# A list planner's cost table and rank offsets replaced: the same instructions of a fused Fourier filter and gated unit in another order

## The chip, the cores and the metric

The kernel runs on one NeuronCore of a Trainium2 chip. The metric is device time in microseconds (us) of one execution, as the median of several. A core has a matrix engine (TensorE, PE in the profile), a vector engine (VectorE, DVE), a scalar engine for activations (ScalarE, ACT), a general engine (GpSimd, POOL) that here starts the loads, and a queue engine (SyncE, SP) that here starts all other transfers. Each engine works off its own list of instructions in the order in which they were written and waits on semaphores; 16 DMA engines move the data. TensorE writes into PSUM, 128 partitions wide; VectorE and ScalarE empty it.

## The reference

Input x has 8 batches of 3200 positions by 256 channels. The first half is a circular filter along the positions, through a real Fourier transform; the second half a causal convolution of five taps per channel, whose sigmoid gates a projection:

```python
X = np.fft.rfft(x, axis=1)
y = np.fft.irfft(X * (filt_r + 1j * filt_i), n=3200, axis=1)
gate = sigmoid(sum(conv_w[k] * y_padded[:, k:k + S, :] for k in range(5)))
out = (gate * (y @ w_val)) @ w_out
```

## The kernel before, in words

The transform of 3200 points is done as 100 times 32, with small matrix products. Per batch the work is cut into these tasks, and a name such as `s1` 2,3 means task 3 of batch 2. In the changed kernel every line number is one higher.

- `lx` (8 per batch): POOL starts a load of 200 KB of x into one of ten buffers (line 200).
- `s1` (8, line 467): PE, transform over 100; `so`: VectorE or ScalarE empties the PSUM tile (lines 458 on ScalarE and 460 on VectorE; these two lines serve `so`, `xs`, `ue` and `oe`).
- `t` (4, line 486): VectorE transposes in blocks of 32.
- `s2` (7, line 496): PE, transform over 32; `xs`: emptied by either engine; `z` (7, line 512): VectorE multiplies by the filter; `ia` (7, line 527): PE, inverse over 32; `ue`: emptied by either engine.
- `wr` (7, line 550) and `lv` (8, lines 560 and 561): SP writes the result to a scratch tensor in DRAM, `escr`, and reads it back as tile `vt`, with rows and partitions exchanged. Every `lv` of a batch waits for all seven `wr` of the batch. Batch 0 alone does this with VectorE transposes instead (`k`, line 568).
- `ib` (8, line 578): PE, inverse over 100; `ye` (8, line 587): ScalarE empties it into `yt`.
- `cv` (7, line 627; the last, quarter-wide one line 613): PE, the convolution as five diagonal products. It needs all eight `ye` of its batch. Two neighbouring pieces are one task with two PSUM slots. `ga` (7, line 637): ScalarE, sigmoid.
- `vl` (7, line 647): PE, the projection; `gv` (7, line 662): VectorE, gate times projection; `op` (7, line 670): PE, the output projection; `oe`: emptied by either engine; `st` (7, line 685): SP stores 512 KB.

The last `s2`, `xs`, `z`, `ia` and `ue` task of a batch is half as wide, the last `cv`, `ga`, `vl`, `gv`, `op`, `oe` and `st` a quarter as wide. PSUM has four slots of this size, and each PE task holds one (a pair of `cv` two) until it is emptied. There are four `gt` and four `gv` buffers, four output buffers, one `u`, one `vt`.

What order the tasks have is not written by hand. A planner (class `Plan`) lists all tasks with the engine and time that each is reckoned to take, their dependencies, buffers and a rank, and lets the time run: whenever an engine is free, the ready task of the lowest rank takes it, and a task that two engines can do goes to whichever takes it. The rank is made of the tables `LAG`, `FIRST` and `STEP`:

```python
return t0 + LAG[stage] + (FIRST.get(stage, 0) if b == 0 else 0) + STEP.get(stage, 1) * n
```

with `t0` eight times the batch number. `STAY` is added for PE when a task has another shape of tiles than the last, and `LEAN` for VectorE when ScalarE could do the task too. Transfers are tasks on an engine `DQ` of their own, in the order in which they become ready, taking turns between loads and the rest. The reckoned times only decide the order; in the finished program every engine waits for the real semaphores.

Of the kernel before, what the change touches and what calls it, by code (L numbers as in the profile page):

```python
# [20 lines left out]
NV = 4 * NS  # L21
TURN = (0,)

LAG = dict(lx=-196.5, s1=-215.5, so=-54.5, t=9.5, pd=-50, s2=-219, xs=-44.5, z=193.5, ia=60,
           ue=52.5, k=-194, ib=97, ye=-272, cv=79.5, ga=-241.5, vl=-22, gv=-253.5, op=152,
           oe=-151)
FIRST = dict(lx=-125.5, s1=102, so=31.5, t=257, pd=29, s2=41, xs=-256, z=-217, ia=-4.5, ue=25,
             k=20.5, ib=113, ye=135, cv=-14.5, ga=-103.5, vl=78, gv=-43.5, op=126, oe=145)
CONV = 1.14
STEP = dict(lx=0, s1=2.15, so=0.4, t=0.4, pd=0.3, s2=1.9, xs=0.4, z=0.8, ue=0.2, k=2.2, ib=2.45,  # L30
            ye=0.5, cv=2.4, ga=2, vl=1.15, gv=1.9, op=1.35, oe=0)
STAY, LEAN = 30.5, 87.5
RC = 4
NCH = R // RC
UCH = [(m, min(2, NM - m)) for m in range(0, NM, 2)]
# [104 lines left out]
def kernel(  # L140
# [28 lines left out]
    DQ = D // E  # L169
# [22 lines left out]
    st = {}  # L192
# [4 lines left out]
    def load_x(b, j):  # L197
        xt = xpool.tile([128, RC, D], BF16, name="xt")
        src = x[b].rearrange("(a r) d -> a r d", r=R)[:, RC * j:RC * j + RC, :]
        nc.gpsimd.dma_start(out=xt[0:L], in_=src)  # L200
        st["X", b, j] = xt
# [490 lines left out]
    add = plan.add  # L692
# [1 line left out]
    def two(a, v):  # L694
        return {"ACT": a, "DVE": v}

    def dma(name, us, rank, dep, give=(), land=2.0):
        add(name, {"DQ": us}, rank, dep, None, land=land, mode=0)
        add(name + "+", {"none": 0.0}, rank, [name], None, give=give)

    for b in range(B):
        turned = b in TURN
        t0 = NCH * b

        def at(stage, n=0, b=b, t0=t0):
            return t0 + LAG[stage] + (FIRST.get(stage, 0) if b == 0 else 0) + STEP.get(stage, 1) * n

        for j in range(NCH):
            if b:
                add(f"lx{b},{j}", {"POOL": 0.6}, at("lx", j), ["hold"],  # L710
                    lambda e, b=b, j=j: load_x(b, j), take=("xt",), land=1.5)
                add(f"dx{b},{j}", {"DQ": 1.15}, at("lx", j), [f"lx{b},{j}"], None, land=2.0, mode=1)
            dep = [f"dx{b},{j}"] if b else [f"x0{j}", "cfa"]
            dep = dep + ([f"s1{b},{j - 1}"] if j else [])
            add(f"s1{b},{j}", {"PE": 0.45}, at("s1", j), dep, lambda e, b=b, j=j: s1(b, j),
                ps=1, take=("so",) if j == 0 else (), give=("xt",), mode=0)
            add(f"so{b},{j}", two(0.93, 1.14), at("so", j), [f"s1{b},{j}"],
                lambda e, b=b, j=j: so(b, j, e), free=[(f"s1{b},{j}", 0)])
        for q in range(4):
            add(f"t{b},{q}", {"DVE": 1.17}, at("t"), [f"so{b},{j}" for j in range(NCH)]  # L720
                + ([f"t{b},{q - 1}"] if q else []),
                lambda e, b=b, q=q: turn(b, q), take=("t",) if q == 0 else (),
                give=("so",) if q == 3 else ())
        add(f"pd{b}", {"POOL": 1.2} if turned else {"none": 0.0}, at("pd"),
            ["pool"] + ([f"pd{b - 1}"] if b else []),
            lambda e, b=b: pad(b), take=("u",) if turned else ("u", "e"))
        for u, (m0, nm) in enumerate(UCH):
            half = 0 if m0 + nm <= FCUT[0][1] else 1
            add(f"s2{b},{u}", {"PE": 0.11 * nm}, at("s2", u), ["wa"]
                + [f"t{b},{q}" for q in range(4)] + ([f"s2{b},{u - 1}"] if u else []),  # L730
                lambda e, b=b, u=u: s2(b, u), ps=1, take=("xs", "z"),
                give=("t",) if u == len(UCH) - 1 else (), mode=1)
            add(f"xs{b},{u}", two(0.13 + 0.4 * nm, 0.04 + 0.55 * nm), at("xs", u),
                [f"s2{b},{u}"], lambda e, b=b, u=u: xs(b, u, e), free=[(f"s2{b},{u}", 0)])
            add(f"z{b},{u}", {"DVE": 0.06 + 0.55 * nm}, at("z", u), [f"xs{b},{u}", f"fl{half}"],
                lambda e, b=b, u=u: zed(b, u), give=("xs",))
            add(f"ia{b},{u}", {"PE": 0.22 * nm}, at("ia", u),
                [f"z{b},{u}", f"te{u // 2},1", f"pd{b}"],
                lambda e, b=b, u=u: inva(b, u), ps=1, give=("z",), mode=1)
            add(f"ue{b},{u}", two(0.13 + 0.4 * nm, 0.04 + 0.55 * nm), at("ue", u),  # L740
                [f"ia{b},{u}"], lambda e, b=b, u=u: ue(b, u, e), free=[(f"ia{b},{u}", 0)])
            if not turned:
                add(f"wr{b},{u}", {"SP": 0.45}, at("ue", u), [f"ue{b},{u}"],
                    lambda e, b=b, u=u: wr(b, u), land=1.0)
                dma(f"wq{b},{u}", 0.38 * nm, at("ue", u), [f"wr{b},{u}"])
        if turned:
            for q in range(4):
                add(f"k{b},{q}", {"DVE": 1.87}, at("k"), [f"ue{b},{u}" for u in range(len(UCH))]
                    + ([f"k{b},{q - 1}"] if q else []),
                    lambda e, b=b, q=q: back(b, q), take=("v",) if q == 0 else (),  # L750
                    give=("u",) if q == 3 else ())
        else:
            add(f"wd{b}", {"none": 0.0}, at("ue"), [f"wq{b},{u}+" for u in range(len(UCH))],
                None, take=("v",), give=("u",))
            for j in range(NCH):
                add(f"lv{b},{j}", {"SP": 0.8}, at("ib", j) - 2, [f"wd{b}"],
                    lambda e, b=b, j=j: lv(b, j), land=1.0)
                dma(f"lq{b},{j}", 0.6, at("ib", j), [f"lv{b},{j}"])
        for j in range(NCH):
            add(f"ib{b},{j}", {"PE": 0.37}, at("ib", j),  # L760
                [f"k{b},3" if turned else f"lq{b},{j}+", "cim"]
                + ([f"ib{b},{j - 1}"] if j else []),
                lambda e, b=b, j=j: ib(b, j), ps=1, take=("y",) if j == 0 else (),
                give=(("v",) if turned else ("v", "e")) if j == NCH - 1 else (), mode=0)
            add(f"ye{b},{j}", {"ACT": 0.79}, at("ye", j), [f"ib{b},{j}"],
                lambda e, b=b, j=j: ye(b, j), free=[(f"ib{b},{j}", 0)])
        add(f"ha{b}", {"POOL": 0.2}, at("ib"), [f"ye{b},0"], lambda e, b=b: halo(b))
        for c in range(NB):
            f = width(c) / BLK
            if c == NB - 1:  # L770
                add(f"cv{b},{c}", {"PE": 0.28}, at("cv", c),
                    [f"ye{b},{j}" for j in range(NCH)] + [f"ha{b}", "dg0", "dg1"],
                    lambda e, b=b, c=c: conv(b, c), ps=1, take=("g",), mode=1)
            elif c % 2 == 0:
                add(f"cv{b},{c}", {"PE": CONV}, at("cv", c),
                    [f"ye{b},{j}" for j in range(NCH)] + [f"ha{b}", "dg0", "dg1"],
                    lambda e, b=b, c=c: conv(b, c), ps=2, take=("g", "g"), mode=2)
            p = c // 2 * 2
            add(f"ga{b},{c}", {"ACT": 0.77 * f + 0.16}, at("ga", c), [f"cv{b},{p}"],
                lambda e, b=b, c=c: gate(b, c), free=[(f"cv{b},{p}", c % 2)])  # L780
            add(f"vl{b},{c}", {"PE": 0.87 * f}, at("vl", c),
                [f"cv{b},{p}"] + ([f"vl{b},{c - 1}"] if c else []), lambda e, b=b, c=c: val(b, c),
                ps=1, take=("gv",), give=("y",) if c == NB - 1 else (), mode=0)
            add(f"gv{b},{c}", {"DVE": 1.08 * f + 0.06}, at("gv", c),
                [f"vl{b},{c}", f"ga{b},{c}"], lambda e, b=b, c=c: gv(b, c), give=("g",),
                free=[(f"vl{b},{c}", 0)])
            add(f"op{b},{c}", {"PE": 0.88 * f}, at("op", c), [f"gv{b},{c}"],
                lambda e, b=b, c=c: outp(b, c), ps=1, take=("o",), give=("gv",), mode=0)
            add(f"oe{b},{c}", two(0.77 * f + 0.16, 1.08 * f + 0.06), at("oe", c),
                [f"op{b},{c}"], lambda e, b=b, c=c: oe(b, c, e), free=[(f"op{b},{c}", 0)])  # L790
            add(f"st{b},{c}", {"SP": 0.5}, at("oe", c), [f"oe{b},{c}"],
                lambda e, b=b, c=c: store(b, c), land=1.0)
            dma(f"sq{b},{c}", 1.2 * f, at("oe", c), [f"st{b},{c}"], give=("o",))
    add("pool", {"none": 0.0}, -100, [], None, land=20.0)
    add("wts", {"POOL": 5.0}, 8.5, ["hold"], lambda e: load_w())
    for j in range(NCH):
# [65 lines left out]
```

## Time and profile before

| what | value |
|---|---|
| three runs | 312.55, 313.03 and 317.41 us; median 313.03 |
| the profiled execution | 311.8 us |
| its span | 310.0 us, so 1.8 us lie around the span |
| mean granted TensorE clock | 0.963 |
| instructions in the span | 10810 |
| HBM | 42.54 MB read, 38.14 MB written |

Busy time of an engine is the time in which some instruction of it runs. Two instructions that follow each other without a pause overlap a little, so the step from one to the next is shorter than the duration of one. The DMA share is the mean busy share of the 16 DMA engines.

### The profile page before, as it was taken

The page shows a single profiled execution, that of the slowest core. Times are in us where ns is not written, and L with a number is a line of the kernel's source. Part 1 is how long each engine was busy: PE and PEld are TensorE (multiplying, and loading weights), DVE is VectorE, ACT ScalarE, POOL GpSimd, SP SyncE. Part 2 cuts the span into 40 slices and gives each one's busy share as a digit, 9 for nine tenths or more (in the row PEclk, how much of TensorE's full clock was granted, in tenths as well). Part 3 has the DMA queues.
Part 4 walks back from the last instruction along what each step waited for, and adds up shares of the span by engine and source line. Part 5 has one row for each costly group of instructions (what it writes and reads, how often), then busy time and mean ns, then how long its engine had stood idle before and what let it go on. Part 6 is the DMA issues. An engine that isn't in the chain of part 4 may idle for free.

```text
span 310.0 us, 10810 instructions
## 1 busy us (share of the span) xinstructions
PE 253.6 (82%) x4616; PEld 157.5 (51%) x4644; DVE 265.0 (85%) x294; ACT 244.9 (79%) x291; POOL 59.4 (19%) x123
## 2 busy tenths in 40 slices
PE   2832779788986799998959969999899989899992
PEld 0121516344544535664547336655666556667661
DVE  7789898899896979999979968999999999285672
ACT  3963889997895888899959957997878789869652
POOL 8773658510230032002300400000000000000000
PEclk9999986999997699999999998999999999999998
DMA  6998699999799969957999978963874789785656
GB/s 98 182 188 157 101 174 123 165 194 239 252 220 243 326 147 239 289 205 171 196 276 327 241 145 266 293 224 118 259 242 164 270 261 294 260 286 191 262 221 237
DMA packets 53520, 67.79 MB, mean 219 GB/s; under 512 B 7840, under 2 KB 34336, under 8 KB 53472
## 3 DMA queue, kind: packets, MB, share of 16 engines
q1 hardware_dynamic: 41264, 51.79, 50.3%
q0 software_dynamic: 12208, 15.31, 31.0%
q8 instruction: 36, 0.59, 0.7%
q14 instruction: 12, 0.10, 0.1%
HBM read 42.54 MB, written 38.14 MB: 260 GB/s over the span
## 4 chain that ended last, share of the span: by engine, by line
PE 34%; DMA 23%; DVE 20%; ACT 8%; issue 7%; POOL 4%; SPq 2%; DVEq 0%; ACTq 0%; POOLq 0%
DMA vt<-escr 9%; PE ps L647 8%; PE ps L670 8%; DMA xt<-in_x_dram 7%; PE ps L627 7%; DVE z L512 6%; DVE gv L662 5%; PE ps L578 4%; PE ps L527 3%; DVE tt L486 3%; PE ps L467 3%; POOL xt L200 2%; ACT gt L637 2%; DVE xs L460 2%; DMA f_t<-in_filt_i_dram 2%
## 5 line engine op out<-in xcount | busy, mean ns | idle before, releaser
L662 DVE TENSOR_TENSOR gv<-ps,gt 128x1024 bf16<-128x1024 f32 (+1 forms) x56 | 61.1, 1103 | 13.0 <-PE ps L647 11.2
L637 ACT ACTIVATE gt<-ps 128x1024 bf16<-128x1024 f32 (+1 forms) x56 | 50.0, 935 | 18.2 <-PE ps L627 16.8
L512 DVE TENSOR_TENSOR z<-xs,f_t 128x2048 bf16<-128x2048 bf16 (+1 forms) x56 | 62.6, 1141 | 0.5 <-ACT xs L458 0.2
L587 ACT ACTIVATE yt<-ps 128x800 bf16<-128x800 f32 x64 | 51.8, 851 | 8.2 <-PE ps L578 5.9
L670 PE MATMUL ps<-wo_t,gv 128*128 128x256 bf16 x400 | 52.0, 274 | 6.5 <-issue 5.2
L200 POOL DMA_DIRECT2D xt<-in_x_dram x64 | 35.4, 557 | 100.8 <-PE ps L467 93.1
L467 PE MATMUL ps<-xt,cf_t 100*128 100x512 bf16 x128 | 44.0, 433 | 12.3 <-DMA xt<-in_x_dram 8.0
L647 PE MATMUL ps<-yt,wv_t 128*128 128x512 bf16 (+1 forms) x196 | 51.4, 356 | 2.2 <-ACT gt L637 0.4
L458 ACT ACTIVATE u<-ps 128x1024 bf16<-128x1024 f32 (+1 forms) x39 | 39.0, 1009 | 12.2 <-PE ps L527 7.9
L670 PEld LDWEIGHTS <-gv 128*128 128x128 bf16 x400 | 37.5, 98 | 16.3 <-issue 9.3
L458 ACT ACTIVATE so<-ps 128x1024 bf16<-128x1024 f32 x39 | 38.8, 1040 | 5.7 <-PE ps L467 5.3
L486 DVE STREAM_TRANSPOSE tt<-so 128x1024 f32<-128x1024 f32 x32 | 39.0, 1234 | 2.0 <-ACT so L458 2.0
L578 PE MATMUL ps<-ci_t,vt 104*128 104x100 f16 (+1 forms) x512 | 35.0, 219 | 7.1 <-DMA vt<-escr 5.2
L458 ACT ACTIVATE xs<-ps 128x1024 bf16<-128x1024 f32 (+1 forms) x38 | 35.9, 975 | 5.5 <-PE ps L496 5.0
L527 PE MATMUL ps<-z,a_t 64*64 64x256 bf16 x416 | 30.5, 309 | 9.7 <-DVE z L512 9.0
L627 PE MATMUL ps<-yt,dg_t 32*32 32x512 bf16 x1920 | 35.9, 387 | 3.1 <-issue 1.3
L578 PEld LDWEIGHTS <-vt 104*128 104x128 bf16 (+1 forms) x512 | 29.3, 104 | 16.7 <-DMA vt<-escr 6.5
L458 ACT ACTIVATE o<-ps 128x1024 f32<-128x1024 f32 (+1 forms) x34 | 32.7, 973 | 6.2 <-PE ps L670 5.0
L460 DVE CAST so<-ps 128x1024 bf16<-128x1024 f32 x25 | 30.1, 1226 | 3.5 <-PE ps L467 3.2
L460 DVE COPY o<-ps 128x1024 f32<-128x1024 f32 (+1 forms) x22 | 22.7, 1033 | 12.0 <-PE ps L670 12.0
L627 PEld LDWEIGHTS <-dg_t 32*32 32x32 bf16 x1920 | 24.1, 88 | 14.5 <-issue 11.0
L496 PE MATMUL ps<-tt,w_t 64*64 64x256 bf16 x416 | 22.8, 298 | 8.8 <-DVE tt L486 5.8
(98 smaller groups left out, 209.6 us busy)
## 6 DMA issues: line engine op xcount, KB each, us to landing
out_dram<-o SPq DMA_DIRECT2D x48, 512.0 KB
xt<-in_x_dram POOLq DMA_DIRECT2D x64, 200.0 KB, 7.7
escr<-u SPq DMA_DIRECT2D x42, 256.0 KB
vt<-escr SPq DMA_DIRECT2D x56, 192.0 KB
out_dram<-o SPq DMA_DIRECT2D x8, 128.0 KB
f_t<-f_t SPq DMA_DIRECT2D x4, 224.0 KB
escr<-u SPq DMA_DIRECT2D x7, 128.0 KB
vt<-escr SPq DMA_DIRECT2D x56, 16.0 KB
```

Of the source, the lines that this page charges most:

```text
L458: nc.scalar.activation(dst, src, AF.Copy, **kw)
L460: nc.vector.tensor_copy(dst, src)
L467: nc.tensor.matmul(ps[:, 512 * h:512 * h + 512], lhsT=cf_t[0:L].rearrange("p h c i -> p (h c i)"), rhs=xv[:, DQ // 2 * h:DQ // 2 * h + DQ ...
L486: nc.vector.transpose(dst, src)
L512: nc.vector.tensor_tensor(z[:, :, :, 0:nm * D], st.pop(("XS", b, u))[:, :, 0:nm * D].unsqueeze(1) .to_broadcast((128, 2, 2, nm * D)), f_t[ ...
L578: nc.tensor.matmul(ps[:, o:o + L], lhsT=v[rows, RC * j + a, 128 * dh:128 * dh + 128], rhs=ci_t[rows, way, :], start=True, stop=True)
L587: nc.scalar.activation(y[:, :, H:H + N].rearrange("p h (a r) -> p h a r", r=R)[:, :, :, RC * j:RC * j + RC], ps[:, :].rearrange("p (h n) - ...
L627: nc.tensor.matmul(two[s][o:o + 32, 512 * dh:512 * dh + BLK], lhsT=dg_t[rows, dh, k, 32 * (i % 2):32 * (i % 2) + 32], rhs=y[rows, dh, p:p ...
L637: nc.scalar.activation(g[:, :, 0:w], two_banks(ps, w), AF.Sigmoid)
L647: nc.tensor.matmul(ps[:, 512 * eh:512 * eh + w], lhsT=wv_t[:, dh, eh, o:o + 128], rhs=y[:, dh, H + BLK * c:H + BLK * c + w], start=(dh == ...
L662: nc.vector.tensor_tensor(o, i0, i1, op=ALU.mult)
L670: nc.tensor.matmul(ps[:, D * a:D * a + D], lhsT=gv_[:, eh, 128 * a:128 * a + 128], rhs=wo_t[:, c % 2, eh, :], start=(eh == 0), stop=(eh == 1))
```

## The change

Nothing is added or taken away: the same matmuls, tiles, loads and stores. The cost table of the planner gets other times for transfers (a load 1.22 instead of 1.15, `wr` 0.44 per half instead of 0.38, `lv` 0.68 instead of 0.6, a store 1.35 instead of 1.2, landing 2.3 instead of 2.0), `CONV` is 1.2 instead of 1.14, and all offsets are other numbers:

```diff
-LAG = dict(lx=-196.5, s1=-215.5, so=-54.5, t=9.5, pd=-50, s2=-219, xs=-44.5, z=193.5, ia=60,
-           ue=52.5, k=-194, ib=97, ye=-272, cv=79.5, ga=-241.5, vl=-22, gv=-253.5, op=152,
-           oe=-151)
-FIRST = dict(lx=-125.5, s1=102, so=31.5, t=257, pd=29, s2=41, xs=-256, z=-217, ia=-4.5, ue=25,
-             k=20.5, ib=113, ye=135, cv=-14.5, ga=-103.5, vl=78, gv=-43.5, op=126, oe=145)
-CONV = 1.14
-STEP = dict(lx=0, s1=2.15, so=0.4, t=0.4, pd=0.3, s2=1.9, xs=0.4, z=0.8, ue=0.2, k=2.2, ib=2.45,
-            ye=0.5, cv=2.4, ga=2, vl=1.15, gv=1.9, op=1.35, oe=0)
-STAY, LEAN = 30.5, 87.5
+LAG = dict(lx=-483.5, s1=-502, so=-78.5, t=229.5, pd=-88, s2=-43.5, xs=8.5, z=246.5, ia=176.5,
+           ue=177.5, k=-247.5, ib=250.5, ye=-415, cv=169, ga=-359, vl=-112.5, gv=-318.5, op=258,
+           oe=-181)
+FIRST = dict(lx=-97.5, s1=161.5, so=44.5, t=431, pd=68.5, s2=193, xs=-429.5, z=-282, ia=9,
+             ue=10.5, k=218.5, ib=167.5, ye=240, cv=25.5, ga=-153, vl=175, gv=-64.5, op=293.5,
+             oe=245)
+CONV = 1.2
+STEP = dict(lx=0.15, s1=2.35, so=1.55, t=1.9, pd=2.2, s2=1.45, xs=2.5, z=1.5, ia=0.2, ue=2.1,
+            k=0, ib=0.3, ye=1.85, cv=0.45, ga=0.85, vl=2.4, gv=0.1, op=1.65, oe=2.05)
+STAY, LEAN = 32.5, 120.5
...
-    def dma(name, us, rank, dep, give=(), land=2.0):
-        add(name, {"DQ": us}, rank, dep, None, land=land, mode=0)
+    def dma(name, us, rank, dep, give=(), land=2.3, mode=0):
+        add(name, {"DQ": us}, rank, dep, None, land=land, mode=mode)
...
-                add(f"dx{b},{j}", {"DQ": 1.15}, at("lx", j), [f"lx{b},{j}"], None, land=2.0, mode=1)
+                add(f"dx{b},{j}", {"DQ": 1.22}, at("lx", j), [f"lx{b},{j}"], None, land=2.0, mode=1)
...
-                dma(f"wq{b},{u}", 0.38 * nm, at("ue", u), [f"wr{b},{u}"])
+                dma(f"wq{b},{u}", 0.44 * nm, at("ue", u), [f"wr{b},{u}"])
...
-                dma(f"lq{b},{j}", 0.6, at("ib", j), [f"lv{b},{j}"])
+                dma(f"lq{b},{j}", 0.68, at("ib", j), [f"lv{b},{j}"])
...
-            dma(f"sq{b},{c}", 1.2 * f, at("oe", c), [f"st{b},{c}"], give=("o",))
+            dma(f"sq{b},{c}", 1.35 * f, at("oe", c), [f"st{b},{c}"], give=("o",))
```

What the planner makes of it, as it stands in the built programs. Up to the end of `ib` of batch 0 (PE), of `t` of batch 1 (VectorE) and of `ye` of batch 0 (ScalarE) both orders are the same. Then the changed order does `s2` and `ia` of batch 1 before the first `cv` of batch 0 is over. From the first `cv` of batch 1 it repeats itself, four times without any difference (digits are task numbers; `cv`, `vl`, `op` and their followers are of batch b, `ib` and `ye` of b+1, `s2` to `ue` of b+2, `s1`, `so` and `t` of b+3, for b = 1 to 4):

```
PE   cv:0 s1:0 vl:0 s1:1 vl:1 s1:2 s2:0 s1:3 s2:1 s1:45 s2:2 s1:67 cv:24 ia:0 s2:3 ia:12 s2:45 op:0
     ib:0 vl:2 ib:1 op:1 ia:3 vl:3 s2:6 cv:6 ia:4 ib:2 op:2 ib:3 vl:4 ia:5 ib:4 op:3 ib:5 vl:5 ib:6
     op:4 ia:6 vl:6 ib:7 op:56
DVE  so:0 gv:01 xs:012 z:012 ue:0 xs:3 ue:2 xs:5 z:3 gv:2 z:4 gv:3 t:0 z:5 oe:2 gv:4 t:1 z:6 gv:5 t:2
     gv:6 t:3 oe:6
ACT  ga:01 so:1234567 ga:2345 ue:1 xs:4 oe:0 ye:01 oe:1 ue:3 xs:6 ga:6 ue:4 ye:23 ue:5 ye:4 oe:3 ye:56
     oe:4 ue:6 ye:7 oe:5
SP   lv:01234567 (b+1) wr:012 st:01 wr:34 st:2 wr:5 st:34 wr:6 st:65
```

Before, no two batches had the same order, and SP's list mixed `lv` of one batch with `wr` and `st` of others. The loads of x for batch b+4 follow `s1` of b+3 in both. Two tasks fall out of the pattern: `op` 0,5 and `op` 0,6 of batch 0 now come at the very end (after `op` 5,3 and after `op` 7,6), and until then their inputs hold two of the four `gv` buffers.

Which engine empties PSUM changes too:

| emptied by | `so` | `xs` | `ue` | `oe` | all |
|---|---|---|---|---|---|
| VectorE, before | 25 | 18 | 17 | 22 | 82 |
| VectorE, after | 9 | 31 | 15 | 20 | 75 |
| ScalarE, before | 39 | 38 | 39 | 34 | 150 |
| ScalarE, after | 55 | 25 | 41 | 36 | 157 |

## The prediction

> **What bounds the kernel now.** The page first: who is busy, what the transfers cost, what the chain of the end is made of.
>
> ```profile
> span 310.0 us, 10810 instructions
> ...
> PE 253.6 (82%) x4616; PEld 157.5 (51%) x4644; DVE 265.0 (85%) x294; ACT 244.9 (79%) x291; POOL 59.4 (19%) x123
> ...
> q1 hardware_dynamic: 41264, 51.79, 50.3%
> q0 software_dynamic: 12208, 15.31, 31.0%
> ...
> PE 34%; DMA 23%; DVE 20%; ACT 8%; issue 7%; POOL 4%; SPq 2%; DVEq 0%; ACTq 0%; POOLq 0%
> ```
>
> No engine is full over the whole span, and the chain is a third transfers and VectorE together with a third TensorE: a pipeline whose bound changes. So I cut the span where both orders have a landmark: the end of the last common stretch, the first `cv` of batch 1, that of batch 4, that of batch 5.
>
> ```profile
> core 0: us, PE busy (x) PEld busy (x) DVE busy (x) ACT busy (x) POOL busy (x), PEclk, DMA share, GB/s
> 0.00:54.30 54.30, 32.07 (x316) 15.91 (x316) 45.59 (x89) 38.56 (x54) 36.55 (x76) 0.94 0.90 146
> 54.30:106.30 52.00, 41.47 (x724) 24.92 (x727) 46.07 (x43) 44.25 (x50) 10.04 (x20) 0.93 0.96 233
> 106.30:213.80 107.50, 95.09 (x1760) 57.48 (x1764) 98.98 (x94) 91.30 (x107) 12.60 (x26) 0.97 0.82 224
> 213.80:239.60 25.80, 23.93 (x556) 16.75 (x566) 25.60 (x24) 20.80 (x27) 0.10 (x1) 1.00 0.67 226
> 239.60:310.00 70.40, 61.00 (x1302) 42.49 (x1279) 48.74 (x48) 49.98 (x58) 0.10 (x1) 0.98 0.72 252
> ```
>
> Four regimes. From 54 to 106 the DMA engines are at 0.96 and nobody else is full. From 106 to 214 VectorE is 92% busy (98.98 of 107.5), with 8.5 us idle. To 239.6 it is full (25.60 of 25.80). Behind that TensorE leads (61.0 of 70.4) and VectorE idles 21.7 us. What VectorE waits for in the two middle regimes shows in the chain:
>
> ```profile
> 84.90 10.54 DMA vt<-escr
> ...
> 146.72 4.43 DMA escr<-u
> 151.17 5.90 DMA vt<-escr
> 157.09 6.71 DMA vt<-escr
> 164.16 3.25 DMA vt<-escr
> ```
>
> Twice the round trip through the scratch tensor holds the chain: 10.5 us from 84.9, 20.3 us in four pieces from 146.7. The landmarks themselves:
>
> ```profile
> 107.06 2.36 PE L627 MATMUL ps<-yt,dg_t 32*32 32x512 bf16 x80
> ...
> 239.27 1.40 PE L627 MATMUL ps<-yt,dg_t 32*32 32x512 bf16 x80
> ```
>
> Batch 1's `cv` starts at 107.1, batch 5's at 239.3; 132.2 us lie between them and 70.7 behind.
>
> **The change, stage by stage.** The work is the same, so the sums need the step of an instruction when its engine is never idle. VectorE's from a stretch without a pause:
>
> ```profile
> 48.69 4.62 DVE L486 STREAM_TRANSPOSE tt<-so 128x1024 f32<-128x1024 f32 x4 [1.16 <-ACT so L458]
> ...
> 205.58 0.67 DVE L512 TENSOR_TENSOR z<-xs,f_t 128x1024 bf16<-128x1024 bf16 x1
> 206.17 1.21 DVE L460 CAST so<-ps 128x1024 bf16<-128x1024 f32 x1
> ...
> 208.43 0.41 DVE L662 TENSOR_TENSOR gv<-ps,gt 128x256 bf16<-128x256 f32 x1
> 208.76 1.22 DVE L512 TENSOR_TENSOR z<-xs,f_t 128x2048 bf16<-128x2048 bf16 x1
> ...
> 219.68 1.21 DVE L460 CAST u<-ps 128x1024 bf16<-128x1024 f32 x1
> 220.81 1.22 DVE L460 CAST xs<-ps 128x1024 bf16<-128x1024 f32 x1
> ```
>
> From 219.68 to 220.81 is 1.13 us, and four transposes in 4.62, the last of them 1.2, give the same: 1.13 for a full tile, whatever the operation; a half `z` steps 0.59 (205.58 to 206.17), a quarter tile 0.33. ScalarE's:
>
> ```profile
> 162.58 0.59 ACT L458 ACTIVATE xs<-ps 128x512 bf16<-128x512 f32 x1
> 163.05 1.03 ACT L458 ACTIVATE u<-ps 128x1024 bf16<-128x1024 f32 x1
> ...
> 268.70 1.94 ACT L637 ACTIVATE gt<-ps 128x1024 bf16<-128x1024 f32 x2 [0.31 <-PE ps L627]
> ...
> 279.79 3.10 ACT L587 ACTIVATE yt<-ps 128x800 bf16<-128x800 f32 x4
> ```
>
> A full tile steps 0.92 (1.94 for two, the second ending 1.02 after its start), a `ye` 0.75 (3.10 less a last 0.84, by three), a half tile 0.47; for a quarter I take 0.33 as on VectorE.
>
> *To 53.3 us* nothing differs on any engine: the four `t` of batch 1 end at 48.69 + 4.62.
>
> *53.3 to the first `cv` of batch 1.* The changed order gives VectorE 40 full tiles, two halves and a quarter here: 40 x 1.13 + 2 x 0.59 + 0.33 = 46.7. Without a pause that ends at 100.0; at the 88.6% of today (46.07 of 52.0) at 106.0. ScalarE has 37 full tiles, eight `ye`, four halves and a quarter: 42.3, so it is not the bound. What can go is the wait of 10.54. Today three stores of batch 0 stand on SP ahead of the first `lv` of batch 1 and a fourth between them; now it is one. A store is 0.524 MB, and the hardware queue moved 51.79 MB in 0.503 x 310.0 = 155.9 us of all engines, 3.01 us per MB: 1.58 per store, three of them 4.7 us. The last `ue` of batch 1 also comes ahead of `ga` 0,2 and 0,3 instead of behind them, so the last `wr` starts no later. The loads of x stay where they are, and they hold most of the DMA share here, so I do not take the whole wait as gone: the middle of both bounds, 103.0, which is 4.1 earlier than 107.1 and less than the 4.7. Bounds 100.0 and 107.
>
> *The four equal cycles.* Per cycle VectorE has 25 full tiles, a half and two quarters: 28.25 + 0.59 + 0.66 = 29.5. ScalarE has 23 full tiles, eight `ye`, two halves, a quarter: 21.2 + 6.0 + 0.9 + 0.3 = 28.4. The table of who empties what is thus nearly even: seven tiles fewer on VectorE in the whole kernel, 7 x 1.13 = 7.9 us off the engine that is full from 106 to 240. The DMA engines have 8 loads (1.64 MB; the software queue took 0.310 x 310.0 = 96.1 us for 15.31 MB, 6.28 per MB: 10.3) and, on the hardware queue, 3.28 MB of stores, 1.70 written to and 1.70 read from `escr` (6.68 x 3.01 = 20.1): 30.4 in the first three cycles. The fourth has no loads: 20.1.
>
> So in cycles 1 to 3 the DMA engines are the longest by a little, and at the highest share that the trace shows over such a stretch, 0.96, a cycle is 31.7. In the fourth VectorE is, at 96%, between its 92% and its 99% above: 30.8. Sum 3 x 31.7 + 30.8 = 125.9, against 132.2. Bounds: from below VectorE alone at 99%, 4 x 29.8 = 119; from above today's own pace. That is 132.2 and 1.4, since the new cycles also hold some three tiles to empty (of `op` 4,4 to 4,6 and `ia` 6,5 and 6,6) that today stand behind the second landmark, on two engines: 133.6.
>
> Why a cycle may get so close to its longest resource: in it the round trip has room. `ue:6` of b+2 ends with the cycle; all eight `lv` are issued first thing in the next, with the stores of b just issued; and the first `ye` has 16 full tiles ahead of it on ScalarE, 14.7 us. The loads of x run in the same half, the `wr` and the stores in the other. Covered that way, moving them costs nothing; if the cover goes, see the second rival.
>
> *From the first `cv` of batch 5.* Today 70.7. The changed list has `op` 0,5 and 0,6 more and `op` 4,4 to 4,6 and two `ia` fewer on TensorE, which leads here; the end has the same chain `op`, `oe`, store, with a quarter tile more. I take 70, bounds 67.5 and 72.
>
> **Sum:** 103.0 + 125.9 + 70 = 298.9, 11.1 below the span of 310.0. The profiled execution, 311.8, becomes 300.7. The median of the runs is 1.2 above it: **302**.
>
> **The rivals.**
>
> *Lock-step.* Four resources at 28 to 30 us per cycle, TensorE in order and four PSUM slots hinder each other, and a cycle takes today's pace, 133.6 for four: 103.0 + 133.6 + 70 + 3.0 = 309.6 (3.0 are the 1.8 around the span and the 1.2 to the median). For it: today VectorE is only full while ScalarE has slack (20.80 of 25.80). Against it: there too the order was fixed and the slots were four.
>
> *The transfers set the pace, and end slower than before.* Place: the loads of x and the `lv` in the first half of cycles 1 to 3. If the DMA engines get no further than the 0.82 that they had from 106 to 214, each of these cycles is 30.4 / 0.82 = 37.1: 103.0 + 3 x 37.1 + 30.8 + 70 + 3.0 = 318.1, and 319.3 or more at 0.81. It decides from a share of 0.86 on: there the cycles take 137 and nothing is gained. For it: the waits at 84.9 and 146.7 are of this kind. Against it: they came while VectorE or a late `ue` let the DMA engines run empty in between, and 0.96 was held for 52 us. The Trainium skill, page "DMA: Bandwidth & Descriptors", section "Issuing engines are not separate DMA queues", says that transfers started by different engines share the same 16 DMA engines and interleave, and that starting them from several saves issue time alone. By this no order of SP and POOL makes a cycle shorter than its transfers, which is this rival; the 0.96 with both queues at work agrees.
>
> *Better still:* the cycles run at VectorE's 99% and the first stage without a pause: 100.0 + 119 + 70 + 3.0 = 292.
>
> That the order is not what the change says is no rival here: the lists are as told, and a load, `wr`, `lv` and store by the queue rows cost 1.29, 0.79, 0.64 and 1.58, near the new table's 1.22, 0.88, 0.68 and 1.35 but for the store.
>
> **How the numbers follow.** Forecast, 295 to 307: 0.50. Better, below 295: 0.07. Lock-step, 307 to 317: 0.28. Transfers, 317 and more: 0.15. About 2% is what a measurement of this kernel tells from no change: faster is below 306.8, slower above 319.3. Faster 0.50 + 0.07 less the forecast's edge, 0.55; slower is most of the transfers' case, 0.13; within, 0.32. The range for 8 in 10 takes in lock-step: 294 to 316; the forecast's own is 295 to 307.
>
> **What would show it.** The first `cv` of batch 1 near 103 instead of 107.1. Four starts of a first `cv` 31 to 32 us apart, the DMA share near 0.95 in three of them, VectorE at 92% or more in all. No piece of the chain on `vt<-escr` longer than 3 us there. 70 us behind the fifth. Wrong it would be with ScalarE and VectorE both near 88% in the cycles (lock-step), or `ib` waiting for `vt` in each (transfers), or a longer tail, because `ib` of batch 7 waits for a later `ue`.

## The result, and the profile after

The changed kernel took 307.74 us, the median of four runs (306.93 to 309.99), beside 314.96 us for the kernel before (four runs). The ratio is 0.987, with a 95% interval from 0.982 to 0.992: 1.3% less time, where 3.5% were forecast, and less than the 2% that the prediction took for no change. Executions of a kernel fall into a faster and a slower state; the ratios, here and in all that follows, count only runs in the faster one, the medians count all. The profiled execution is the slowest of the four, 309.99 us with a span of 308.1. Its page:

```profile
span 308.1 us, 10833 instructions
...
PE 254.9 (83%) x4644; PEld 154.1 (50%) x4644; DVE 261.0 (85%) x287; ACT 248.9 (81%) x298; POOL 59.5 (19%) x123
...
q8 instruction: 36, 0.59, 0.8%
...
PE 43%; DVE 11%; issue 6%; ACT 4%; DMA 2%; SPq 1%; ACTq 0%; DVEq 0%
```

VectorE lost 4 us of work and ScalarE gained 4, the way that the table of who empties what says, but half of the 7.9 us that the prediction took from it: the seven tiles were counted there as full ones, and five of them are half as wide. In the chain of the end the transfers fell from 23% to 2%, but the changed kernel's chain reaches back only to some 99 us. From 100 us on the chain of before has 23 us of transfers, all on the way through the scratch tensor, and that of the changed kernel a single piece, in the third cycle:

```profile
179.13 6.54 DMA vt<-escr
```

The chain puts it ahead of a `ga` on ScalarE at 185.7, which does not read `vt`; ScalarE worked without a pause there (5.67 us from 178.16, 3.77 from 183.88), so it held nothing up. In the kernel before, TensorE's `ib` waited for the round trip through the scratch tensor, 5.2 us in total, five times, 3.1 us at the longest:

```profile
PE ps L578 <- DMA vt<-escr: 5.2, 5, 3.1
```

The changed kernel's table of waits has no such entry. The same cuts as in the prediction, by engine busy time, clock and DMA share, with the first `cv` of a batch (103.76 for batch 1) as the landmark where a cycle begins:

```profile
core 0: us, PE busy (x) PEld busy (x) DVE busy (x) ACT busy (x) POOL busy (x), PEclk, DMA share, GB/s
0.00:54.30 54.30, 30.84 (x306) 14.52 (x306) 44.87 (x88) 36.93 (x51) 35.15 (x73) 0.87 0.89 142
54.30:103.90 49.60, 40.78 (x751) 22.75 (x766) 46.91 (x44) 46.06 (x54) 11.58 (x23) 1.00 1.00 234
103.90:138.30 34.40, 31.40 (x590) 19.26 (x590) 30.51 (x28) 28.39 (x35) 4.53 (x9) 0.95 0.87 245
138.30:173.50 35.20, 31.18 (x590) 19.34 (x583) 29.98 (x29) 29.31 (x35) 4.53 (x9) 0.95 0.84 238
173.50:206.30 32.80, 29.78 (x590) 18.31 (x604) 30.13 (x29) 29.20 (x35) 3.53 (x8) 1.00 0.83 245
206.30:238.20 31.90, 30.00 (x590) 18.09 (x599) 29.94 (x29) 29.18 (x35) 0.10 (x1) 1.00 0.63 212
238.20:308.10 69.90, 60.97 (x1308) 41.84 (x1297) 48.70 (x46) 49.81 (x59) 0.11 (x1) 1.00 0.68 242
```

Two of the three forecast terms hold: the first cycle starts at 103.8 (103.0), and 69.9 us lie behind the fourth (70). The four cycles between took 34.4, 35.2, 32.8 and 31.9, together 134.3 instead of 125.9. They are 2.1 us longer than the stretch that they replace (132.2): what the profiled execution gained lies ahead of them, where the first `cv` of batch 1 starts 3.3 us earlier than before, and behind them, 0.7 us. In each cycle every engine does the same instructions, and VectorE and ScalarE are busy for nearly the same time, yet the lengths differ by 3 us. The fourth, which has no loads of x, is the shortest.

What TensorE waited for in the second cycle, from the table of waits and from its timeline:

```profile
PE ps L628 <- issue: 3.6, 1, 3.6
PE ps L468 <- DVE xs L461: 0.2, 1, 0.2
```

```profile
147.72 1.96 PE L628 MATMUL ps<-yt,dg_t 32*32 32x512 bf16 x101
153.27 0.62 PE L628 MATMUL ps<-yt,dg_t 32*32 32x512 bf16 x23 [3.59 <-issue]
```

In the middle of `cv:4` TensorE stops for 3.59 us, and the page's word for the cause is "issue": nothing that it shows. Every cycle has 1156 instructions of TensorE, and the other cycles have such a stop too: the fourth four matmuls earlier in its list than the second, the first and the third some 65 matmuls later, in `ia`:

```profile
117.90 0.30 PE L528 MATMUL ps<-z,a_t 64*64 64x256 bf16 x3
120.00 0.37 PE L528 MATMUL ps<-z,a_t 64*64 64x256 bf16 x1 [1.79 <-issue]
...
187.11 0.30 PE L528 MATMUL ps<-z,b_t 64*64 64x256 bf16 x3
189.15 0.27 PE L528 MATMUL ps<-z,b_t 64*64 64x256 bf16 x1 [1.74 <-issue]
...
214.87 2.79 PE L628 MATMUL ps<-yt,dg_t 32*32 32x512 bf16 x133
218.31 0.64 PE L628 MATMUL ps<-yt,dg_t 32*32 32x512 bf16 x27 [0.65 <-issue]
```

Such a stop lies between two matmuls that read the same tiles, so a wait for data is an unlikely cause. Two things in the trace name another. First, the place: counting all of TensorE's instructions in the trace in order and from 0 (9351: weight loads, matmuls and the few waits), the first one after each of the four stops is number 2753, 3777, 5057 and 6081, and after a fifth of 0.62 us in the last stage 7617. Each is 193 more than a multiple of 256. Second, the DMA queue "instruction" of the page, q8: 36 packets, 0.59 MB, is 16 KB a packet, and 9351 instructions in 36.5 blocks of 256 are 64 bytes each. The number of packets goes with the number of instructions in the experiments below too: 37 for the 9455 of `shift`, 29 for the 7431 of `half`. In the window from 150.9 to 152.0, inside the longest stop:

```profile
q0 software_dynamic: 83, 0.15, 74.6%
q1 hardware_dynamic: 59, 0.09, 24.8%
q8 instruction: 1, 0.02, 6.1%
```

One such packet moves, among 83 packets of the loads of x; TensorE goes on 1.27 us after it ends. By the DMA records of the trace each block has one packet, and none starts more than 0.6 us before TensorE enters the block in front; so I take that entry for the request, which itself leaves no record. For the blocks behind the four stops the packet starts 3.67, 3.62 and 3.46 us after it in cycles 1 to 3, with loads under way, and 0.71 us after it in the fourth, which has none. So TensorE's instructions come by the same DMA engines as the data; with loads under way such a block is in use 5.7 to 6.2 us after its request, without them 3.0; and `cv:2 cv:4`, 320 instructions in 3.0 us (112.5 to 115.5 in cycle 1, where no stop falls into it), use a block up faster. The Trainium skill, page "Runtime: NRT & Kernel Launch", section "Terms", says that each engine's instruction memory is refilled in blocks of 16 KiB, which agrees with the 36 packets; what it costs here is read from these runs.

### The profile page after: what moved, and what is told of

Its sections match the earlier page's. It is cut to its first block, busy times and chain, and to the rows that moved or that the text cites. A ratio compares the mean times of both kernels' runs of the same rounds, so it can differ in the third digit from the quotient of the medians.

```text
span 308.1 us, 10833 instructions
## 1 busy us (share of the span) xinstructions
PE 254.9 (83%) x4644; PEld 154.1 (50%) x4644; DVE 261.0 (85%) x287; ACT 248.9 (81%) x298; POOL 59.5 (19%) x123
## 4 chain that ended last, share of the span: by engine, by line
PE 43%; DVE 11%; issue 6%; ACT 4%; DMA 2%; SPq 1%; ACTq 0%; DVEq 0%
PE ps L671 14%; PE ps L648 9%; PE ps L628 7%; PE ps L579 4%; DVE gv L663 4%; PE ps L528 4%; PE ps L468 2%; DMA vt<-escr 2%; DVE xs L461 2%; ACT o L459 2%; PE ps L497 2%; DVE z L513 1%; DVE o L461 1%; DVE so L461 1%; DVE u L461 1%
## 5 line engine op out<-in xcount | busy, mean ns | idle before, releaser
L459 ACT ACTIVATE so<-ps 128x1024 bf16<-128x1024 f32 x55 | 53.7, 1029 | 9.4 <-PE ps L468 8.6
L468 PE MATMUL ps<-xt,cf_t 100*128 100x512 bf16 x128 | 44.7, 443 | 11.5 <-DMA xt<-in_x_dram 8.1
L648 PE MATMUL ps<-yt,wv_t 128*128 128x512 bf16 (+1 forms) x224 | 52.3, 356 | 1.1 <-ACT gt L638 0.5
L528 PE MATMUL ps<-z,a_t 64*64 64x256 bf16 x416 | 30.4, 300 | 16.2 <-DVE z L513 10.5
L459 ACT ACTIVATE o<-ps 128x1024 f32<-128x1024 f32 (+1 forms) x36 | 34.8, 974 | 8.2 <-PE ps L671 8.1
L461 DVE CAST xs<-ps 128x1024 bf16<-128x1024 f32 (+1 forms) x31 | 36.1, 1183 | 1.8 <-PE ps L497 1.8
L579 PE MATMUL ps<-ci_t,vt 104*128 104x100 f16 (+1 forms) x512 | 33.7, 212 | 1.1 <-ACT o L459 0.6
L528 PE MATMUL ps<-z,b_t 64*64 64x256 bf16 x416 | 30.1, 292 | 2.4 <-issue 2.4
L628 PEld LDWEIGHTS <-dg_t 32*32 32x32 bf16 x1920 | 22.6, 88 | 17.8 <-issue 13.5
L528 PEld LDWEIGHTS <-a_t 64*64 64x64 f16 x416 | 15.8, 112 | 29.0 <-DVE z L513 14.8
L497 PE MATMUL ps<-tt,w_t 64*64 64x256 bf16 x416 | 23.7, 303 | 7.8 <-DVE tt L487 5.6
```

The lines of the kernel that those rows point to most:

```text
L459: nc.scalar.activation(dst, src, AF.Copy, **kw)
L461: nc.vector.tensor_copy(dst, src)
L468: nc.tensor.matmul(ps[:, 512 * h:512 * h + 512], lhsT=cf_t[0:L].rearrange("p h c i -> p (h c i)"), rhs=xv[:, DQ // 2 * h:DQ // 2 * h + DQ ...
L528: nc.tensor.matmul(ps[64 * h:64 * h + 64, 512 * t + D * a:512 * t + D * a + D], lhsT=tab[rows, h, m0 + a, :], rhs=z[rows, w, h, D * a:D * ...
L579: nc.tensor.matmul(ps[:, o:o + L], lhsT=v[rows, RC * j + a, 128 * dh:128 * dh + 128], rhs=ci_t[rows, way, :], start=True, stop=True)
L628: nc.tensor.matmul(two[s][o:o + 32, 512 * dh:512 * dh + BLK], lhsT=dg_t[rows, dh, k, 32 * (i % 2):32 * (i % 2) + 32], rhs=y[rows, dh, p:p ...
```

## The experiments

The length of each cycle and, in brackets, the time that TensorE stood dry in it (the entries "issue" in its timeline, 0.3 us and more), from the profiled run of each. A cycle is cut at the first `ga` of a batch here, for the changed kernel's first profile at the first `cv`; the lengths differ by less than 0.1 us.

| run | cycle 1 | cycle 2 | cycle 3 | cycle 4 | sum | time, median | to the kernel before, 95% |
|---|---|---|---|---|---|---|---|
| changed kernel | 34.4 (1.79) | 35.2 (3.59) | 32.8 (1.74) | 31.9 (0.65) | 134.3 | 307.74 | 0.987, 0.982 to 0.992 |
| again | 32.1 (0.86) | 36.0 (3.55) | 35.8 (2.56) | 31.4 (0) | 135.3 | 310.14 | 0.987, 0.974 to 1.001 |
| again5 | 31.9 (0.78) | 35.7 (3.55) | 34.4 (2.05) | 31.7 (0.49) | 133.7 | 311.32 | 0.989, 0.975 to 1.002 |
| shift | 36.3 (3.65) | 32.8 (1.89) | 33.5 (2.40) | 31.1 (0) | 133.7 | 309.36 | 0.991, 0.987 to 0.995 |
| noload | 31.3 (0) | 32.0 (0.84) | 30.9 (0) | 31.9 (0.62) | 126.1 | 299.90 | 0.967, 0.953 to 0.980 |
| half | 34.0 (0) | 33.7 (0) | 33.7 (0) | 33.6 (0) | 135.0 | 319.58 | 1.026, 1.018 to 1.035 |
| later | 32.7 (0) | 34.2 (1.14) | 31.3 (0) | 31.9 (0.43) | 130.1 | 307.03 | 0.988, 0.976 to 1.000 |
| later_home | 35.6 (0) | 35.5 (0) | 31.5 (0.42) | 31.8 (0) | 134.4 | 308.33 | 0.989, 0.979 to 0.999 |
| part | 31.3 (0) | 34.2 (2.25) | 31.4 (0.37) | 31.5 (0) | 128.4 | 304.54 | 0.979, 0.969 to 0.989 |
| soon | 31.3 (0) | 32.8 (1.35) | 31.3 (0) | 31.7 (0.37) | 127.1 | 302.28 | 0.974, 0.965 to 0.983 |

Runs of one kernel scatter by up to 7 us here, the changed one as well as the one before, so the cycles say more than the medians.

**The changed kernel again**, unchanged, in two sets of runs, `again` and `again5`.

> The changed kernel once more, for a second profile. Three theories of why the four equal cycles took 34.4, 35.2, 32.8 and 31.9 us instead of the forecast 31.7 and 30.8. Fetch: TensorE's own instructions come in packets of 16 KB, a block of 256; the next block is asked for when the last one is entered, and it came 6.0 us later in the cycles with loads of x, while cv:2 and cv:4 alone are 320 instructions in 2.6 us, so TensorE ran dry for 1.8, 3.6 and 1.7 us. Transfers: the data transfers of a cycle are late. Lock-step: four evenly loaded engines hinder each other. Fetch expects idle time of TensorE that ends with nothing the profile shows at the same instructions, with sizes that vary by a us or two; transfers expects waits of ib for vt; lock-step expects cycles of one length, loads or not.

> The changed kernel, as the reference on this chip for the two runs that follow: 307 to 310 us, cycles of 31.4 to 36, dry times of TensorE of 1 to 4 us in cycles 1 to 3.

The stops are at the same places of the program, in cycles 1 to 3, and their sizes move by up to a microsecond: cycle 1 has 1.79 in one run and 0.78 in another. A cycle's length goes with its dry time; the profile of the second set:

```profile
103.30:135.20 31.90, 29.92 (x575) 18.32 (x574) 30.00 (x28) 29.21 (x34) 4.54 (x9) 1.00 0.92 264
135.20:170.90 35.70, 31.22 (x577) 18.88 (x576) 29.90 (x28) 29.37 (x34) 4.54 (x9) 0.95 0.83 236
170.90:205.30 34.40, 31.32 (x575) 19.22 (x575) 30.16 (x28) 29.40 (x35) 3.54 (x8) 0.95 0.80 232
205.30:237.00 31.70, 29.98 (x578) 18.06 (x580) 29.91 (x28) 29.14 (x34) 0.10 (x1) 1.00 0.64 214
```

The first cycle, with all its loads and the DMA engines at 0.92, takes hardly longer than the fourth: its dry time is short this time. Lock-step expected one length for all; it is out.

**The same program, 104 TensorE instructions later.**

```diff
-        for m in range(m0, m1):
+        for m in [*range(m0, m1), *range(m0, m1)]:
             for h, t in ((0, 0), (1, 1), (0, 1), (1, 0)):
```

> The small matrix products that make the tables at the start are issued twice, 104 more TensorE instructions in a stretch where TensorE idles; all else is the same. Fetch: every border of a block of 256 falls 104 instructions earlier in the same work, so from the traced starts the dry times become 3.8 us in cycle 1 (1.8 before), 2.0 in cycle 2 (3.6 to 3.9), 3.9 in cycle 3 (1.7 to 2.0) and none in cycle 4 (0.7 to 1.0): cycles of 36.4, 33.3, 34.7 and 31.2, time between 307 and 311. Transfers and lock-step: the cycles stay at 34.4, 35.2, 32.8, 31.9, and no idle time changes its place.

The dry times came out at 3.65, 1.89, 2.40 and none, where 3.8, 2.0, 3.9 and none had been worked out; the cycles at 36.3, 32.8, 33.5 and 31.1, for 36.4, 33.3, 34.7 and 31.2. Cycle 1's stop moved into `cv:4`:

```profile
111.97 1.25 PE L628 MATMUL ps<-yt,dg_t 32*32 32x512 bf16 x67
116.87 0.63 PE L628 MATMUL ps<-yt,dg_t 32*32 32x512 bf16 x9 [3.65 <-issue]
```

and cycle 2's out of it, behind `ia:1`. Nothing but the place of the borders between blocks was changed in these cycles, so the borders make the stops: the first instruction after each of the three is again 193 more than a multiple of 256. One size was off: 2.40 for 3.9 in cycle 3. The time, 309.36, was in the expected 307 to 311.

**Without the loads of cycles 1 to 3.**

```diff
     def load_x(b, j):
+        if b > 4:
+            st["X", b, j] = st["held", j]
+            return
...
-        st["X", b, j] = xt
+        st["X", b, j] = st["held", j] = xt
```

> Left out: the loads of x for batches 5, 6 and 7, which run in cycles 1 to 3; these batches are computed from batch 4's x instead. Same instructions on TensorE, VectorE and ScalarE, same order. Fetch: with the DMA engines less full the packet starts about 1 us after it is asked for, as in cycle 4, instead of 3.6; dry times of at most 1.2 us, all cycles about 31.9, time 6 to 7 us less, 301. Transfers: the same sum, but the gain shows as waits for data that are gone. Lock-step: the cycles stay at 33 to 35, time 306 or more.

```profile
102.90:134.20 31.30, 29.83 (x575) 18.20 (x574) 29.92 (x28) 29.08 (x35) 0.10 (x1) 1.00 0.64 216
134.20:166.20 32.00, 29.92 (x575) 18.04 (x574) 29.94 (x28) 29.12 (x34) 0.10 (x1) 1.00 0.62 211
166.20:197.10 30.90, 29.77 (x578) 18.15 (x576) 29.91 (x28) 29.07 (x34) 0.10 (x1) 1.00 0.64 218
197.10:229.00 31.90, 30.03 (x580) 18.11 (x582) 29.93 (x28) 29.16 (x35) 0.10 (x1) 1.00 0.64 213
```

All four cycles are now within 1.1 us of each other, 126.1 together. That this is near the forecast's 125.9 is chance, for the forecast reckoned with the loads. They cost the changed kernel's cycles 8 us, and the tables of waits of its cycles had no wait for data; what is gone is all but 1.5 us of the dry times. It does not yet tell whether the loads act through the instruction packets alone.

**Half the instructions in the convolution.** (In `val` and `outp` the turn by `c % 2`, which undid the turn of the 32-wide tiles, goes too.)

```diff
-                for i in range(4):
-                    rows = slice(32 * i, 32 * i + 32)
-                    o = 32 * ((i + n) % 4)
-                    nc.tensor.matmul(two[s][o:o + 32, 512 * dh:512 * dh + BLK],
-                                     lhsT=dg_t[rows, dh, k, 32 * (i % 2):32 * (i % 2) + 32],
+                for i in range(2):
+                    rows = slice(64 * i, 64 * i + 64)
+                    o = 64 * (i ^ dh)
+                    nc.tensor.matmul(two[s][o:o + 64, 512 * dh:512 * dh + BLK],
+                                     lhsT=dg_t[rows, dh, k, :],
```

> The convolution of a full pair is done with 64x64 tiles instead of 32x32: 40 matmuls and 40 weight loads instead of 80 and 80, at about 2.2 us instead of 1.3 for a pair; the same result. Fetch: cv:2 and cv:4 are now 160 instructions in 4.4 us, and TensorE no longer runs dry: 1.8, 3.6 and 1.7 us gone in cycles 1 to 3, against up to 0.9 us more for each of three pairs a cycle that ScalarE may wait for: cycles of 32.5 to 34, time 303 to 309. Transfers and lock-step: nothing gained and 1 to 2.7 us lost per batch, time 313 to 325.

With the loads in place and the DMA engines at 0.86, no dry time is left anywhere: with fewer instructions per microsecond a late packet (3.3 us after the entry in cycle 1) is still in time. But the price was more than the upper end that I gave it: cycles of 33.7 without any dry time are 2.4 us over the 31.3 of the run without loads, and 2.6% over the kernel before in all. ScalarE waits for the longer `cv` 13 times in four cycles, 12.8 us by its table of waits (7.0, 7 times, in the changed kernel):

```profile
ACT gt L638 <- PE ps L628: 12.8, 13, 2.0
```

The cycles together, 135.0, are hardly longer than the changed kernel's 134.3; most of the loss in time lies behind them, where the stretch from the first `cv` of batch 5 takes 78.4 us instead of 70. The time, 319.58, falls into what the other two theories expected, 313 to 325, but the dry times, which tell the theories apart, are gone as Fetch expected. So the 32-wide tiles are the better choice here, although they are what makes the instructions dense.

**The loads moved out of the dense half.** POOL waits for a `ga` of the running batch before it starts the loads of the batch four ahead; the order of every engine stays. In `later` the last six loads wait for `ga:4`, in `part` the last three, in `soon` the last six wait for `ga:2`.

```diff
     def load_x(b, j):
+        if b > 4 and j == 2:
+            late = g1.tile([128, 1], BF16, name="late")
+            nc.gpsimd.tensor_copy(late[...], st["G", b - 4, 4][:, 0, 0:1])
         xt = xpool.tile([128, RC, D], BF16, name="xt")
```

> Same order on every engine; POOL waits for ga:4 of the running batch before it starts the last six loads of the batch four ahead (and with them the first two of the next), so that the loads no longer run while TensorE works off s1, s2 and the three pairs of cv. Fetch: the packets of TensorE's instructions come about 3.2 us after they are asked for in that half, dry times of at most 1.2 us, cycles of 31.3 to 32.3 as without loads, provided the loads still land before s1 of the next cycle: 4 to 7 us less than the changed kernel, 301 to 304. Transfers: 30 us of transfers have less room than before, the loads or the stores come late and the cycles stay at 34 or more. Lock-step: no change within 1%.

> As the run with later loads, but only the last three loads of a batch, and the first two of the next, wait for ga:4; the other three run with s1. The later loads took the dry times away and gave most of it back as waits of oe for an output buffer whose store had not landed. If both are a matter of how many transfers share the time, this has dry times of about 1 us and waits on stores of under 1 us: cycles of 31.5 to 33, 2 to 4 us less than the changed kernel. If any load in the first half delays the packets fully, the dry times stay at 2 to 3.6 and there is nothing gained.

> As the run with later loads, but POOL waits for ga:2 instead of ga:4, so the loads start some 2 us earlier, when cv:2 is done and cv:4 runs. The packet for the block behind cv:4 is asked for about then. If what counts is the queue of loads ahead of a packet, the dry times are at most 1.5 us and the stores land 2 us sooner than with the later loads: 2 to 4 us less than the changed kernel.

`later` took the dry times away but for 1.14 us in cycle 2 and 0.43 in cycle 4, yet its time, 307.03, is within 1 us of the changed kernel's 307.74: the expected 301 to 304 was wrong. Its chain shows where the gain went, to a store that frees an output buffer:

```profile
153.99 1.03 ACT o L471
155.02 0.02 issue
155.04 12.66 DMA out_dram<-o
```

The loads now run with the stores, a store takes 12.7 us to land, and `oe:4` on ScalarE waits 1.4 us for it; `oe:6` on VectorE waits 2.5 us for another one. `part` and `soon` share the time better. `part` has cycles of 31.3 to 31.5 but for one of 34.2, with a dry time of 2.25 where about 1 was expected; by the ratios, 0.979 for 0.989, it takes 3 us less than the changed kernel in its set, as expected. `soon` has cycles of 31.3, 32.8, 31.3 and 31.7:

```profile
104.40:135.70 31.30, 29.83 (x575) 18.20 (x574) 29.65 (x27) 29.05 (x35) 5.41 (x10) 1.00 0.89 242
135.70:168.50 32.80, 29.97 (x575) 18.09 (x575) 30.09 (x28) 29.22 (x34) 5.33 (x10) 1.00 0.94 270
168.50:199.80 31.30, 29.71 (x575) 18.22 (x576) 30.35 (x29) 29.12 (x34) 4.34 (x9) 1.00 0.90 262
199.80:231.50 31.70, 30.03 (x578) 18.12 (x582) 29.93 (x28) 29.18 (x35) 0.11 (x1) 1.00 0.66 223
```

All loads are there, the DMA engines are at 0.89 to 0.94 in the first three, above the 0.83 to 0.87 of the changed kernel, and the cycles are nearly as short as without loads, 127.1 together for 126.1. Some packets of instructions are as late as ever, 3.5 and 3.6 us in the second half of cycle 1, but where TensorE is slow to use up a block, and no stop follows. In cycle 1 of `part` the DMA engines are at 0.97, and it takes 31.3 us too. This rules out the transfers' own time as the cause: the same loads, 7 to 10 us later in the cycle, cost 1 us in four cycles instead of 8 (2.0 us of waits for a store remain on VectorE). `soon` takes 0.974 of the kernel before (0.965 to 0.983). By the ratios, 0.974 for 0.989, it takes 4.5 us less than the changed kernel of the same set, a little more than the expected 2 to 4; the two intervals overlap, but its cycles are 6.6 us shorter in the profiles.

**The two stray tasks put back**, with the later loads.

```diff
+    move("PE", "op0,5", "op0,4")
+    move("PE", "op0,6", "op0,5")
+    move("DVE", "oe0,5", "oe0,4")
+    move("ACT", "oe0,6", "ue2,6")
+    move("SP", "st0,5", "st0,4")
+    move("SP", "st0,6", "st0,5")
```

> As the run with later loads, and op 0,5 and op 0,6 with their oe and st stand behind op 0,4 instead of at the end, which gives the two held gv buffers back. If these buffers or the tail mattered, this is over 1 us faster than the later loads alone; if not, as I think, 0 to 0.7 us, for the quarter tile at the very end moves to the first cycle's start.

No gain: 308.33 beside 307.03, within the scatter. Its first two cycles took 35.6 and 35.5 with no dry time, waiting for output buffers as above (the chain has one store of 13.84 us there), so the two stores more at that place do not help. The stretch behind the fourth cycle is 1 us shorter (69.1 instead of 70.2 from the first `cv` of batch 5). What the held `gv` buffers cost in the changed kernel itself, without the later loads and their waits, was not tested.

**One part of the change alone.** `offsets_only` has the new offsets with the old times of transfers and `cv`; `costs_only` the old offsets with the new times.

> The new offsets, with the old times of the transfers and of cv. The planner makes another order of it: no equal cycles, cv:0 and cv:2 back to back in two batches, transfers of several batches mixed on SP again. If the equal cycles, with room for the round trip, are where the gain over the kernel before comes from, this has waits on vt in the chain again and is no faster than the kernel before, 311 to 320. If the offsets by themselves carry the gain, 305 to 309.

> The old offsets, with the new times of the transfers and of cv: the order stays close to that of before (the first 94 tasks of TensorE are the same), without equal cycles. If the new times by themselves carry the gain, 305 to 309; if it needs offsets searched for them, within 1.5% of the kernel before, 309 to 317.

The new offsets alone took 316.78 us, 1.017 of the kernel before (1.009 to 1.026); the new times alone 312.36, 1.000 (0.995 to 1.006). Neither order has equal cycles, and neither gains: offsets and times belong together. With the offsets alone, TensorE stood dry for 10.6 us, in stops of up to 3.81, while by the table of waits it waited only 0.2 us for `vt`. Its chain reaches back only to 178.6 us; from there to 250 it has 12 us of the round trip (4.2 on `vt`, 7.8 on the writes to `escr`) beside 9.9 of "issue". So the reason that I gave for the loss is borne out in part at most; what made this order slower, beside 2 us more of dry time than in the changed kernel, is not settled.

## Why the prediction was right and wrong

*The way and two terms were right.* The first `cv` of batch 1 came at 103.8 us for 103.0, and the stretch behind the fourth cycle took 69.9 for 70. That the first fits so well is partly luck: 103.0 was the middle of two bounds, the four `t` of batch 1, which end the common stretch, end 1.5 us later in this profile than before (54.8 for 53.3), and in the two other profiles of the changed kernel that `cv` starts at 101.1 and 101.8. VectorE's work per cycle, reckoned at 29.5, was 29.9 to 30.5 by the windows. The round trip has the room that the prediction gave it: no entry of the cycles' tables of waits has `ib` waiting for `vt`. The sign that I named for it, no piece of the chain on `vt<-escr` longer than 3 us, failed with the 6.54 us above, though nothing waited for them.

*The term that failed is the four cycles,* 125.9 for 134.3. It left out that TensorE's instructions come through the DMA engines too. The sentence that failed is the one on the loads of x in the first half of a cycle, "Covered that way, moving them costs nothing": they were covered for the data, and cost the dry stops. The rows of before held the sign of it: 7% of "issue" in its chain, and its trace has two dry stops of 2.6 us, at 156.3 and 182.2, each at a packet of q8.

```profile
PE ps L670 <- issue: 5.2, 2, 2.6
```

I read "issue" as nothing. In the changed kernel the stops are 7.8 us in the four cycles, 1.79, 3.59, 1.74 and 0.65. Without them the cycles are 126.5 by that subtraction, 126.1 in the run without loads, 127.1 with the loads out of the way. By the same subtraction the stretch of before is 127.0 (132.2 less 5.2), so besides the stops the new order gained 0.5 us there, or some 2 with the 1.4 that the prediction reckoned for its extra tiles. The subtraction is rough, for a stop can hide another wait; how much the freed round trip is worth in these cycles stays open.

*The working inside the term was wrong too, though its sum was near.* I took the DMA engines at a share of 0.96 as what sets cycles 1 to 3, at 31.7. They ran at 0.83 to 0.87, and cycles of 31.3 us came with shares of 0.64 and of 0.97 alike: they did not set the pace as a whole. In the cycles without a long stop two engines are nearly full, VectorE (29.94 of 31.9; 29.91 of 30.9 without loads) and TensorE (30.00 and 29.77), whose work per cycle the prediction did not add up. Which of the two sets the pace then, no run tells.

*Lock-step* forecast 309.6 and came closest to the time, for a reason that the runs refute: unhindered cycles take 31.3, not 33.4.

*The transfers' rival* had the right culprit, the loads of x in the first half of cycles 1 to 3, and its point of decision, a share of 0.86, is about where the cycles ran; that says little, since 30.4 us of transfers in a cycle of 34.4 to 35.2 come to such a share whatever made it long. But no data came late. The loads held back TensorE's instructions, 3.5 us or more from request to start instead of 0.7, and that the engines are shared holds for the instruction queue as well, as q8 beside q0 and q1 in one window shows.

*The step on the stray tasks and the buffers* they hold, which I left at nothing but a quarter tile, is not contradicted by any run, nor tested in the changed kernel itself.

## What to carry to other kernels

Instructions of TensorE are a transfer: count them per microsecond, and look in the trace whether a stop marked "issue" falls on a packet of the instruction queue; small tiles in a row, with bulk loads under way, run it dry. An order that is planned from times of data transfers alone may put the bulk loads just where the instructions are densest; a single wait that holds the loads back for 7 to 10 us brought here about as much again as the whole new order (in one set of runs 0.974 of the kernel before, against 0.989 for the order alone). And a regular, repeating schedule has one more use: cycles that should be equal and aren't point at what lies outside the plan.

## What the hardware showed that I had not expected

A block of 256 TensorE instructions seems to be asked for when the block before it is entered: in the changed kernel no packet starts more than 0.6 us before that. The packet follows 0.5 to 2.1 us after the entry in cycle 4, with 0.63 of the DMA engines busy, and 3.5 to 3.7 us after it at the stops of cycles 1 to 3, with loads queued. Loads are not needed for a stop: the fifth, of 0.62 us, lies in the last stage, where its packet came 3.0 us after the entry. The packet itself took 0.9 to 1.6 us; at the five stops TensorE went on 1.3 to 1.6 us after its end.

A dry stop can cost more than its length. Eight times in the cycles of the changed kernel (three profiles), `shift` and `part` the granted TensorE clock falls to 0.50, for 3.4 or 6.8 us, each time at a stop of 1.79 us or more or within 2 us behind it. In the changed kernel and `shift` the cycles with such a fall are 0.4 to 2.0 us longer than 31.2 us and their stops, the others differ from that by at most 0.3 us (31.2 is cycle 4 of the last profile less its own 0.49). The Trainium skill, page "TensorE: Matmul & The Clock Gate", section "What's actually happening", describes a clock that is throttled unless recent activity releases it; these cycles agree, but not every stop has this price: one of 1.74 us in the first profile and those of 1.89 and 2.40 us in `shift` left the clock at 1.00.
